# Attention and long convolution on one core: spacing row loads and instruction blocks in a planned order, with a landing wait on SyncE

## The chip, the core and the metric

The kernel runs on one core of a Trainium2 chip. Its engines work side by side, each through its own instructions in order: TensorE (PE; its weight loads are PEld in a profile), VectorE (DVE), ScalarE (ACT), GpSimd (POOL), and SyncE (SP), which here issues nearly all transfers. Semaphores tie them together. The metric is the device time of one execution in microseconds; lower is better.

## The reference

Two independent results are set side by side in one output of 2048 rows by 1024 columns.

```python
# left half: attention, 2048 positions, 32 heads of 16
qkv = x @ wqkv
p = softmax((q @ k.T) * 16 ** -0.5)          # per head
a = (p @ v) @ wo
# right half: gated long convolution, 512 channels
kv = shift(k, shift_k) * v                   # 4 taps per channel
y = irfft(rfft(pad(kv)) * rfft(pad(ssm_k)))[:2048]   # causal convolution over 2048 positions
b = q * (y + kv * ssm_D)
```

## The kernel before

**Attention.** Scores are made transposed, 128 keys by 512 queries at a time. Such a piece is a *block*; there are 2048 (4 query parts, 8 head groups, 16 key tiles, 4 heads at a time). The program walks through 695 *steps*. In each, TensorE makes the scores of two or three blocks (three in most, two in every other of the first 56 and in the last nine) into two alternating sets of three PSUM banks (`emit_qk`, the matmul at L762). ScalarE takes the exponential of all of them in one instruction (L769, 128x1536 for three blocks, 128x1024 for two). In 308 steps one block goes to VectorE and GpSimd instead, which build the exponential from integer arithmetic in *sets* of two or four blocks (L790 takes the block out of PSUM, L821 and L839 are GpSimd's pieces, L922 to L926 a polynomial, L889 or L894 the finish). TensorE then multiplies by the values (L971) into one of two banks.

**Convolution.** It is done by matmuls against shifted copies of the filter. The filter rows are laid out in a DRAM scratch, `kz_scratch`, and 256 KB of them serve one channel: that is one *row load*, `WR<-kz_scratch`. Four channels make a *quad*; 128 quads are worked off one after the other, each with four row loads into one of four buffers and 16 *lags* of four matmuls (`conv_lags`, L1157). Eight quads make a block of 32 channels, which TensorE then turns (L1178) and VectorE multiplies by q (L1188); after four of those a store goes out, and the next q columns are loaded (`QN`).

**The order.** Nothing is scheduled at run time. While the program is built, a planner in Python gives each engine a clock of its own, adds a duration for every instruction, and writes down each engine's list. Table constants at the top of the file steer it:

- `dve_choice` decides whether a step gives a block to VectorE: `LATE` and `OPEN_LATE` say how far VectorE may be behind, `OPEN_STEPS` how far apart sets are while all are pairs, `FIX_BEHIND` how far VectorE's clock may be past TensorE's, `LAST`, `PAIRS_AT_END` and `ROOM_END` rule the end.
- `V_DUE`, `X1_AT` and `X2_AT` set when the projections of values and queries are due.
- `run_conv` puts lags between score groups. The share that is due follows from what is left and from `CONV_END`. A piece is cut where `pe.stall` expects TensorE to run out of instructions: TensorE's list is taken to arrive in blocks of `FETCH` = 256, each `FETCH_US` after the last at the earliest.
- `load_wr` writes row loads into SyncE's list, one each `PACE` us of the plan's clock, or one each `PACE / 1.5` when more than six are waiting. A load carries a wait for the last TensorE instruction that had been planned then (`hold`), so that SyncE cannot issue it earlier, and for the quad that had used the buffer. The plan reckons when it lands from `START_US`, `SET_US` and `LAND_LATE`; `conv_ready` lets the lags of a quad into the plan only then.

SyncE's list is one queue: what stands behind a load that waits is issued after it.

Of the kernel before, what the change touches and what calls it, by code (L numbers as in the profile page):

```python
# [43 lines left out]
N_EARLY = 56  # L44
LAGS = 5
CONV_AT = 128
CONV_END = 640
TAIL = 18


# [12 lines left out]
TIME = 0.8  # L63
FULL = 4
APART = 2
OPEN_STEPS = 3
ROOM = {2: 4.0, 4: 8.0}
LATE = 9.0
CLOSE = 4.0
LAST = 6  # L70
ROOM_END = 1.5
PAIRS_AT_END = 20
PAIRS_AT = 4
OPEN_LATE = 4.5
DVE_OVER = 0.084
ACT_US = 0.425
ACT_OP = 0.066
DVE_SEEN = 0.12
FIX_BEHIND = 1.8
NEXT = -0.1  # L80
PV_HOLD = 3
LAG_US = 0.068
# [5 lines left out]
FILL_LATE = 0.5  # L88
HARD = 0.7
FETCH = 256  # L90
FETCH_AT = 192
FETCH_US = 4.0
EARLY = 6
ISSUE_US = 0.45
START_US = 2.0
# [4 lines left out]
SET_US = 0.72  # L100
# [3 lines left out]
KZ_AT = 11  # L104
KZ0_AT = 14
DG_AT = (1, 1, 7, 8)
V_DUE = -1
PACE = 0.95
FULL_PARTS = 6
KZ_LANDS = 24.2  # L110
KZ_OVER = 0.0
# [9 lines left out]
MUL_WAIT = 6  # L121
FINISH_RATE = 1.5
PASS_US = 3.0
X2_AT = 146
X1_AT = 166


class Count:
# [13 lines left out]
class Eng:  # L142
# [17 lines left out]
    def stall(self, n, us):  # L160
        (b, landed), late = self.fetch, 0.0
        while self.count + n > b:
            t = self.t + late + us * (b - self.count) / n
            late += max(0.0, landed - t)
            landed = max(landed, t) + FETCH_US
            b += FETCH
        return late, (b, landed)

    def op(self, fn, deps=(), inc=True, us=None, late=FILL_LATE, fill=False, counted=False):
        waits = []  # L170
        ready = max([0.0] + [self.at[(id(d[0]), d[1])] for d in deps if d])
        while self.fill and not fill and self.t + self.fill[0][0] <= ready + late:
            self.fill.pop(0)[1]()
        if inc and (self.sem, self.n) in deps:
            self.tied.add(self.n + 1)
        for d in deps:
            if d is None:
                continue
            sm, v = d
            self.t = max(self.t, self.at[(id(sm), v)])  # L180
            if self.seen.get(id(sm), 0) < v:
                self.seen[id(sm)] = v
                waits.append((sm, v))
        if counted:
            c = Count()
            fn(c)
            n = c.n + max(len(waits) - 1, 0)
            late, self.fetch = self.stall(n, us)
            self.t += late
            self.count += n  # L190
            self.counts = [x for x in self.counts if x[0] > self.t - RATE_US] + [(self.t, n)]
        self.t += (self.us if us is None else us) - (DVE_OVER if self.us == 0.69 else 0.0)
        self.last = [x for x in self.last if x[0] > self.t - SPAN] + [(self.t, self.us if us is None else us)]
        if inc:
            self.n += 1
            self.at[(id(self.sem), self.n)] = self.t + self.seen_after
        self.ops.append((waits, fn, self.sem if inc else None))
        return (self.sem, self.n)
# [21 lines left out]
def bass_concat_heads__mha_block__ssm_conv_h3__prompt_kernel(  # L220
# [21 lines left out]
    def sem(name):  # L242
        return enter(nc.semaphore(name))

    def sb(name, shape, dt=BF16):
# [36 lines left out]
    WR = [WRF[:, o:o + 4 * LROW].rearrange("p (c w) -> p c w", c=4)  # L282
          for o in (0, 4 * LROW + 64, 8 * LROW + 64, 12 * LROW + 96)]
# [15 lines left out]
    pe, act, dve, pool, sp = [Eng(sem(n), at, us, after) for n, us, after in (  # L299
        ("s_pe", 0.5, 0.11), ("s_act", 0.5, 0.16), ("s_dve", 0.69, DVE_SEEN), ("s_pool", 0.5, 0.1), ("s_sp", 0.05, 0.1))]  # L300

    queue = [0.0]

    def dma(eng, dsem, outp, inp, deps=(), transpose=False, us=4.0, takes=0.0):
        h = dsem.add()

        def fn(e):
            f = e.dma_start_transpose if transpose else e.dma_start
            f(outp, inp).then_inc(dsem.sem, 16)
        eng.op(fn, deps, inc=False, us=ISSUE_US if takes else 0.05)  # L310
        if takes:
            queue[0] = max(queue[0], eng.t + START_US) + takes
            us = queue[0] + 0.9 - eng.t
        at[(id(dsem.sem), dsem.n)] = eng.t + us
        return h
# [4 lines left out]
    def when_of(h):  # L320
        return at[(id(h[0]), h[1])] if h else 0.0
# [11 lines left out]
    d_wr = [DmaSem(sem(f"d_wr{i}")) for i in range(R_W)]  # L333
# [3 lines left out]
    wview = A_wqkv.rearrange("(c p) f -> p c f", p=128)  # L337
    h_x = {}
    h_x0 = dma(sp, d_x[0], KVE[:, 0:4, 0:C], x2[0:512, :].rearrange("(t p) d -> p t d", p=128))
    h_wq = [dma(act, d_w[0], WQ[:, :, 0:128], wview[:, :, 0:128])]  # L340
    h_wk = [dma(act, d_w[1], WK[:, :, 0:128], wview[:, :, D:D + 128])]

    def turn_in(dsem, dst, src, deps=(), us=4.0):
# [183 lines left out]
    h_kzt, h_kzs = [None], {}  # L527
# [56 lines left out]
    def k_part(r0, r1):  # L584
        def fn(e):
            ins = None
            for dc in range(4):
                ins = e.matmul(PS[:, 7, r0:r1], lhsT=WK[:, dc, 0:128], rhs=xT[:, dc, r0:r1], start=(dc == 0), stop=(dc == 3))
            return ins
        return pe.op(fn, h_x[0] + [h_wk[0], bank_free[7]], us=0.3 if r0 == 0 else 0.8)  # L590
    h = k_part(0, 128)
# [94 lines left out]
    def dve_choice(T):  # L686
# [3 lines left out]
        j = len(s.blks)  # L690
        if T + (s.k - j) * APART >= NT - LAST or not s.free() or dve.t > pe.t + FIX_BEHIND:
            return None
        behind = max(dve.t + sum(x[0] for x in dve_fill) + PASS_US * len(waiting) - pe.t, 0.0)
        if j == 0 and (behind > (LATE if h_kzall[0] else OPEN_LATE) or s.k == 2 and sets and T - sets[-1].at < OPEN_STEPS and T < FULL_AT) or j and T - s.at < APART * (s.k > 2):
            return None
        if len(rest_of[n]) / 3 < (ROOM[s.k] if T < NT - PAIRS_AT_END else ROOM_END) + APART * (s.k - 1 - j) + behind / 1.25:
            n = max(n + 1, 2)
# [411 lines left out]
    h_wr, h_qn, h_turn, h_yb = {}, {}, {}, {}  # L1109
# [6 lines left out]
    def load_wr(T):  # L1116
        while next_wr[0] < C // 4 and slots:
            qd = next_wr[0]
            next_wr[0] += 1
            r, h = slots.pop(0)  # L1120
            slot_of[qd] = r
            wr_parts.extend((qd, c, r, h) for c in range(4))
        while wr_parts:
            rate = max(RATE, sum(x[1] for x in pe.counts) / RATE_US)
            left = ((FETCH_AT - pe.count) % FETCH) / rate
            if pe.t < next_wr[1] or left < FETCH_NEAR and pe.t < next_wr[1] + 2 * FETCH_NEAR:
                return
            next_wr[1] = max(next_wr[1], pe.t - PACE) + (PACE if len(wr_parts) <= FULL_PARTS else PACE / 1.5)
            hold = [pe_last()] if next_wr[0] > 3 else []
            qd, c, r, h = wr_parts.pop(0)  # L1130
            src = bass.AP(tensor=kz_ap.tensor, offset=kz_ap[4 * qd + c, 0, 0].offset,
                          ap=[[NB * VG, 128 // VG], [LKZ, VG], [1, LROW]])
            h_wr[qd] = dma(sp, d_wr[r], WR[r][:, c, :], src, [h_kzs[i] for i in range(12, 16)] + [h] + hold, takes=SET_US)
            if c == 3:
                land[qd] = when_of(h_wr[qd]) + LAND_LATE

# [60 lines left out]
    def when(qb, g, kt, s=0):  # L1197
        return plan[blk_index[(qb, g, kt, s)]]
# [50 lines left out]
    def turn_job(b):  # L1249
        def job(T, bank):  # L1250
            def run():
# [11 lines left out]
    todo = [(when(0, 0, kt) + 1, x_at[kt // 4], n, unit_job("v", kt, 0, n)) for kt, n in [(0, 1), (1, 1)] + [(i, 2) for i in range(2, KT, 2)]]  # L1263
    todo += [(when(0, 4, kt) + V_DUE, when(0, 3, kt + 1, 3) + 4, 2, unit_job("v", kt, 1, 2)) for kt in range(0, KT, 2)]
    n_unit = 4 // UNIT
# [3 lines left out]
             for c in range(4) for j in range(4)]  # L1269
    todo += [(min(when(qb, 2 * o, 0) - 2 - EARLY, {1: X1_AT, 2: X2_AT}.get(qb, 999) + 8 * o), max(when(qb - 2, 2 * o + 1, 15, 3) + 6 if qb > 1 else 140 + 16 * (o // 2), 0),  # L1270
              n_unit, unit_job("q", qb, o)) for qb in range(1, NQB) for o in range(4)]
# [93 lines left out]
    def bg_step(T, lim):  # L1365
# [17 lines left out]
        if T >= N_EARLY:  # L1383
            st["lags"] = min(st["lags"] + rest / max(CONV_END - T, 1.0), 3.0 * LAGS)
        if run_jobs(T, lim):
# [58 lines left out]
    def pe_last():  # L1444
        return (pe.sem, pe.n)
# [186 lines left out]
```

## Time and profile before

| | us |
|---|---|
| runs | 809.6, 810.16, 813.01 |
| median | 810.16 |
| the profiled execution | 815.64 |
| its span, first to last instruction | 813.8 |
| ScalarE busy | 793.5 (98%) |
| VectorE busy | 771.1 (95%) |
| TensorE busy, matmuls | 704.0 (87%) |
| GpSimd busy | 369.6 (45%) |
| granted TensorE clock, mean | 0.993 |

The profile is one execution, taken apart by the hardware profiler. A group of instructions has its line in the program, its engine, what it writes and reads, how often it occurs, its busy time, and the idle time of the engine just before it with what ended that. L762 and so on are lines of the kernel before. The profiled execution has a time of its own, which is not that of the median run.

### The profile page before, as it was taken

Reading aid. Unit: us, or ns where it says so; the run is one execution under the profiler, and the core shown is the slowest. Engines: PE = TensorE matmul, PEld = TensorE weight load, DVE = VectorE, ACT = ScalarE, POOL = GpSimd, SP = SyncE. Lnnn points to the kernel's source line nnn. Section 1 sums busy time; section 2 is a strip of 40 time slices with the busy share of each in tenths; the row PEclk is TensorE's granted clock in tenths of the full one; section 3 lists DMA queues with packets and bytes.
Section 4 is the critical chain, followed back from the end, with each engine's and each line's share of the span. In section 5 each row is a group of like instructions: output and inputs, shape, how many; then the busy total and the mean of one; then the engine's idle time right before and its main releaser. Section 6 shows DMA issues by size and latency. Waiting matters only on the chain.

```text
span 813.8 us, 30354 instructions
## 1 busy us (share of the span) xinstructions
PE 704.0 (87%) x13322; PEld 317.5 (39%) x13356; DVE 771.1 (95%) x1160; ACT 793.5 (98%) x702; POOL 369.6 (45%) x453
## 2 busy tenths in 40 slices
PE   8988999888888888888888888888888879888887
PEld 3333334232344443434434444343444343344442
DVE  4999999999889999999999999999999989999997
ACT  6999999999999999999999999999999998999997
POOL 4322543465443354665364455455453444444440
PEclk9999999999999999999999999999999998999999
DMA  9976700214367876579878788688678788778851
GB/s 239 305 276 246 190 1 17 61 27 103 106 194 225 269 235 193 172 216 262 282 223 260 252 253 256 192 260 265 205 223 243 247 253 251 242 217 280 267 167 49
DMA packets 125012, 167.33 MB, mean 206 GB/s; under 512 B 50384, under 2 KB 57040, under 8 KB 124624
## 3 DMA queue, kind: packets, MB, share of 16 engines
q1 hardware_dynamic: 122480, 164.34, 66.3%
q8 instruction: 105, 1.72, 0.9%
q10 hardware_dynamic: 2400, 1.05, 0.6%
q14 instruction: 27, 0.22, 0.1%
HBM read 143.14 MB, written 16.52 MB: 196 GB/s over the span
## 4 chain that ended last, share of the span: by engine, by line
ACT 85%; PE 7%; DVE 6%; issue 1%; DMA 1%; DVEq 0%
ACT PT L769 85%; PE PS L762 2%; PE PS L971 1%; DVE EI L790 1%; DMA WR<-kz_scratch 1%; PE PS L1157 1%; PE PS L575 1%; DVE EA L926 1%; DVE EA L924 1%; PE PS L479 0%; PE PS L1082 0%; DVE WR L541 0%; DVE EI L889 0%; DVE KV L515 0%; DVE EA L925 0%
## 5 line engine op out<-in xcount | busy, mean ns | idle before, releaser
L769 ACT ACTIVATE PT<-PS 128x1024 bf16<-128x1024 f32 (+1 forms) x695 | 789.4, 1420 | 8.4 <-PE PS L762 7.9
L762 PE MATMUL PS<-QT,KTo 32*128 32x512 bf16 x2048 | 274.2, 387 | 92.1 <-ACT PT L769 62.3
L971 PE MATMUL PS<-PT,VAF 128*32 128x512 bf16 x1740 | 235.7, 391 | 0.2 <-DVE STG L1041 0.2
L1157 PE MATMUL PS<-WR,KV 128*6 128x64 bf16 (+15 forms) x8192 | 187.2, 213 | 5.6 <-issue 3.8
L1157 PEld LDWEIGHTS PS<-WR,KV 128*26 128x26 bf16 (+15 forms) x8192 | 150.2, 120 | 47.2 <-issue 25.6
L762 PEld LDWEIGHTS PS<-QT,KTo 32*128 32x128 bf16 x2048 | 70.5, 91 | 240.3 <-ACT PT L769 212.9
L790 DVE TENSOR_SCALAR EI<-PS 128x512 int32<-128x512 f32 x228 | 154.7, 681 | 7.0 <-PE PS L762 6.6
L821 POOL TENSOR_SCALAR xT<-EI 128x512 f16<-128x512 uint16 x84 | 78.0, 936 | 89.5 <-DVE xT L894 23.8
L839 POOL TENSOR_SCALAR EI<-EI 128x512 f16<-128x512 uint16 x100 | 76.6, 774 | 54.9 <-DVE EI L889 10.0
L821 POOL TENSOR_SCALAR STG<-EI 128x512 f16<-128x512 uint16 x74 | 64.4, 877 | 72.9 <-DVE EI L894 19.0
L971 PEld LDWEIGHTS PS<-PT,VAF 128*32 128x32 bf16 x1740 | 56.2, 93 | 83.7 <-issue 79.6
L790 DVE TENSOR_SCALAR xT<-PS 128x512 int32<-128x512 f32 x80 | 54.6, 682 | 3.1 <-PE PS L762 2.8
L971 PE MATMUL PS<-EI,VAF 128*32 128x512 bf16 x228 | 56.3, 389 | 0.2 <-DVE STG L1041 0.2
L821 POOL TENSOR_SCALAR STG<-xT 128x512 f16<-128x512 uint16 x34 | 31.5, 934 | 44.0 <-DVE EI L894 15.3
L1334 PE MATMUL PS<-ZR,IDN 128*128 128x512 bf16 (+3 forms) x192 | 51.0, 319 | 0.2 <-DVE EA L925 0.2
L821 POOL TENSOR_SCALAR xT<-xT 128x512 f16<-128x512 uint16 x37 | 31.7, 868 | 42.6 <-DVE EI L894 15.1
L894 DVE SCALAR_TENSOR_TENSOR EI<-EI,EA 128x1024 int16<-128x1024 uint16 (+1 forms) x46 | 46.5, 1022 | 0.3
L924 DVE TENSOR_TENSOR EA<-EA,xT 128x2048 f16<-128x2048 f16 x33 | 40.3, 1223 | 0.4
L926 DVE TENSOR_TENSOR EA<-EA,xT 128x2048 f16<-128x2048 f16 x33 | 40.4, 1223 | 0.2
L925 DVE TENSOR_SCALAR EA<-EA 128x2048 f16<-128x2048 f16 (+2 forms) x60 | 35.1, 586 | 0.8
L926 DVE TENSOR_TENSOR WKV<-WKV,STG 128x2048 f16<-128x2048 f16 x29 | 35.5, 1224 | 0.2
L924 DVE TENSOR_TENSOR WKV<-WKV,STG 128x2048 f16<-128x2048 f16 x29 | 35.3, 1218 | 0.3
(107 smaller groups left out, 700.6 us busy)
## 6 DMA issues: line engine op xcount, KB each, us to landing
WR<-kz_scratch SPq DMA_DIRECT2D x512, 256.0 KB, 3.8
kz_scratch<-WR SPq DMA_DIRECT2D x16, 752.0 KB, 4.5
QN<-in_B_q_dram SPq DMA_DIRECT2D x16, 128.0 KB, 3.5
out_dram<-KV SPq DMA_DIRECT2D x16, 128.0 KB, 4.1
out_dram<-OUTA SPq DMA_DIRECT2D x12, 128.0 KB, 2.7
QT<-in_B_ssm_k_dram SPq DMA_DIRECT2D x1, 1024.0 KB, 5.7
EI<-in_B_ssm_k_dram SPq DMA_DIRECT2D x1, 1024.0 KB, 7.7
STG<-in_B_v_dram SPq DMA_DIRECT2D x1, 1024.0 KB, 6.1
```

The costliest lines, as they stand in the source:

```text
L762: ins = e.matmul(PS[:, bank, :], lhsT=KTo[32 * s:32 * s + 32, g // 2, kt * 128:(kt + 1) * 128], rhs=QT[32 * s:32 * s + 32, qb % 2, g, :], ...
L769: h_exp[T] = act.op(lambda e: e.activation(PT[:, T % R_PT, 0:n * QB], PS[:, banks[0]:banks[0] + n, :].rearrange("p b f -> p (b f)"), ACT.E ...
L790: s.fix.append(dve.op(lambda e: e.tensor_scalar(ei_of(i)[:, 0, :], PS[:, bank, :], FIX_LO, FIX_ADD, ALU.max, ALU.add), [h] + old + [o.pv[i ...
L821: return e.tensor_scalar(out, src.bitcast(UINT16).rearrange("p i (f e) -> p i f e", e=2)[:, :, :, 0], FS / OCT, 0.0, ALU.mult, ALU.add)
L839: return e.tensor_scalar(out.bitcast(FP16)[:, :, 0:QB], src.bitcast(UINT16).rearrange("p i (f e) -> p i f e", e=2)[:, :, :, 1], FS, 0.0, A ...
L894: h = dve.op(lambda e: e.scalar_tensor_tensor(out, whole, FS, m, ALU.mult, ALU.add), [st[i] for i in range(k0, k1)], us=0.155 + 0.533 * (k ...
L924: step(2, lambda sl: lambda e: e.tensor_tensor(ea[:, sl], ea[:, sl], eb[:, sl], ALU.mult))
L925: step(4, lambda sl: lambda e: e.tensor_scalar(ea[:, sl], ea[:, sl], C1, 1.0, ALU.add, ALU.mult))
L926: step(2, lambda sl: lambda e: e.tensor_tensor(ea[:, sl], ea[:, sl], eb[:, sl], ALU.mult))
L971: ins = e.matmul(PS[32 * s:32 * s + 32, pvb(qb * NG + g), :], lhsT=VAF[:, kt, h * VW:h * VW + 32], rhs=rhs, start=(order[b] == 0), stop=(o ...
L1157: ins = e.matmul(PS[32 * c:32 * c + NW - 2 * n, BGB, col:col + 64], lhsT=KV[:, 2 * n:NW, 4 * qd + c], rhs=w, start=(n == 0), stop=(n == NB ...
L1334: return e.matmul(PS[:, bank, col:col + 128 * k], lhsT=IDN[:, :], rhs=ZR[:, :].rearrange("p (m d) -> p m d", m=1).broadcast_to([128, 4 * k ...
```

## The change

Two things change. Thirteen of the planner's constants get other values. The two in the change's name: `FETCH_US`, the least time between two blocks of TensorE's instructions, goes from 4.0 to 4.5, and `PACE`, between two row loads, from 0.95 to 1.1. The others concern the opening (`OPEN_STEPS`, `OPEN_LATE`, `V_DUE`, `X1_AT`, `X2_AT`), how far VectorE may lag (`LATE`, `FIX_BEHIND`), the end (`LAST`, `ROOM_END`, `PAIRS_AT_END`) and the convolution's end (`CONV_END`). And an engine's list can now hold a *soft* wait: it stands in the list and holds the engine on the chip, but the planner's clock does not know of it. `load_wr` uses it: a load of the first two channels of a quad waits until the quad two in front has landed, one of the last two until the quad one in front has.

```diff
-CONV_END = 640
+CONV_END = 647
-OPEN_STEPS = 3
+OPEN_STEPS = 4
-LATE = 9.0
+LATE = 10.0
-LAST = 6
-ROOM_END = 1.5
-PAIRS_AT_END = 20
+LAST = 5
+ROOM_END = 1.0
+PAIRS_AT_END = 18
-OPEN_LATE = 4.5
+OPEN_LATE = 5.0
-FIX_BEHIND = 1.8
+FIX_BEHIND = 1.6
-FETCH_US = 4.0
+FETCH_US = 4.5
-V_DUE = -1
-PACE = 0.95
+V_DUE = 1
+PACE = 1.1
-X2_AT = 146
-X1_AT = 166
+X2_AT = 144
+X1_AT = 162
...
     def op(..., soft=()):
...
+        for sm, v in soft:
+            if self.seen.get(id(sm), 0) < v:
+                self.seen[id(sm)] = v
+                waits.append((sm, v))
...
-            h_wr[qd] = dma(sp, d_wr[r], WR[r][:, c, :], src, [...] + [h] + hold, takes=SET_US)
+            h_wr[qd] = dma(sp, d_wr[r], WR[r][:, c, :], src, [...] + [h] + hold, takes=SET_US,
+                            soft=[h_wr[qd - 1 - (c < 2)]] if qd > 1 else [])
```

Lines are added by the change, so L762 is L766 in it, L1157 is L1162, L309 is L313. What it moves, at three places:

SyncE, the loads behind the fourth load of q columns (some 655 us in the profile before); `d_wr` is the landing of a row buffer. Before:

```order
L309 DMA WR<-kz_scratch 128x1x1024
L309 DMA QN<-in_B_q_dram 128x4x128 [waits s_dve]
L309 DMA QN<-in_B_q_dram 128x4x128 x3
L309 DMA out_dram<-KV 128x4x128
L309 DMA WR<-kz_scratch 128x1x1024 [waits s_pe] x4
L309 DMA out_dram<-KV 128x4x128
L309 DMA WR<-kz_scratch 128x1x1024 [waits s_pe] x5
L309 DMA out_dram<-KV 128x4x128
L309 DMA WR<-kz_scratch 128x1x1024 [waits s_pe] x4
L309 DMA WR<-kz_scratch 128x1x1024
```

Now:

```order
L313 DMA WR<-kz_scratch 128x1x1024 [waits d_wr2]
L313 DMA QN<-in_B_q_dram 128x4x128 [waits s_dve]
L313 DMA QN<-in_B_q_dram 128x4x128 x3
L313 DMA out_dram<-KV 128x4x128
L313 DMA WR<-kz_scratch 128x1x1024 [waits s_pe] x3
L313 DMA WR<-kz_scratch 128x1x1024 [waits d_wr3,s_pe]
L313 DMA out_dram<-KV 128x4x128
L313 DMA WR<-kz_scratch 128x1x1024 [waits s_pe] x2
L313 DMA WR<-kz_scratch 128x1x1024
L313 DMA WR<-kz_scratch 128x1x1024 [waits d_wr0,s_pe]
L313 DMA out_dram<-KV 128x4x128
L313 DMA WR<-kz_scratch 128x1x1024 [waits s_pe] x3
```

One load in four has got the landing wait, the third of its quad (the second pair's other load and the next quad's first two find that landing already waited for), and the stores of KV stand behind it; between two stores there are four row loads instead of four or five.

TensorE, where quad 117 begins (some 742 us before). Its lags fall from 32 columns to 2 within a quad. Before:

```order
L1157 MATMUL PS<-WR,KV 8x64 x4
L1157 MATMUL PS<-WR,KV 6x64 x4
L1157 MATMUL PS<-WR,KV 4x64 x4
L1157 MATMUL PS<-WR,KV 2x64 x4
L1157 MATMUL PS<-WR,KV 32x64 x4
L1157 MATMUL PS<-WR,KV 30x64 x4
L1157 MATMUL PS<-WR,KV 28x64 x4
L1157 MATMUL PS<-WR,KV 26x64 x4
L1157 MATMUL PS<-WR,KV 24x64 x4
L1157 MATMUL PS<-WR,KV 22x64 x4
L762 MATMUL PS<-QT,KTo 128x512 x3
L971 MATMUL PS<-PT,VAF 32x512 x2
```

Now:

```order
L1162 MATMUL PS<-WR,KV 8x64 x4
L1162 MATMUL PS<-WR,KV 6x64 x4
L1162 MATMUL PS<-WR,KV 4x64 x4
L1162 MATMUL PS<-WR,KV 2x64 x4
L1162 MATMUL PS<-WR,KV 32x64 x4
L1162 MATMUL PS<-WR,KV 30x64 x4
L1162 MATMUL PS<-WR,KV 28x64 x4
L1162 MATMUL PS<-WR,KV 26x64 x4
L1162 MATMUL PS<-WR,KV 24x64 x4
L1162 MATMUL PS<-WR,KV 22x64 x4
L766 MATMUL PS<-QT,KTo 128x512 x3
L975 MATMUL PS<-PT,VAF 32x512 x4
```

The last four lags of a quad and the first six of the next stand between two groups of scores in both; the row loads and the steps around them are spaced differently, the piece itself is not.

VectorE, the last sets before the closing transposes. Before:

```order
L925 TENSOR_SCALAR EA<-EA 128x2048
L926 TENSOR_TENSOR EA<-EA,xT 128x2048
L894 SCALAR_TENSOR_TENSOR EI<-EI,EA 128x2x512 x2
L821 TENSOR_SCALAR EA<-EI 128x512 x2
L922 TENSOR_SCALAR EA<-EA 128x512 x2
L924 TENSOR_TENSOR EA<-EA 128x512 x2
L925 TENSOR_SCALAR EA<-EA 128x512 x2
L926 TENSOR_TENSOR EA<-EA 128x512 x2
L894 SCALAR_TENSOR_TENSOR EI<-EI,EA 128x512 x2
L1061 STREAM_TRANSPOSE STG<-PS 128x256
```

Now:

```order
L929 TENSOR_SCALAR EA<-EA 128x512 x2
L930 TENSOR_TENSOR EA<-EA 128x512 x2
L898 SCALAR_TENSOR_TENSOR EI<-EI,EA 128x512 x2
L825 TENSOR_SCALAR xT<-EI 128x512
L926 TENSOR_SCALAR EA<-xT 128x2048
L928 TENSOR_TENSOR EA<-EA,xT 128x2048
L929 TENSOR_SCALAR EA<-EA 128x2048
L930 TENSOR_TENSOR EA<-EA,xT 128x2048
L898 SCALAR_TENSOR_TENSOR EI<-EI,EA 128x2x512 x2
L1065 STREAM_TRANSPOSE STG<-PS 128x256
```

Before, a set of four finished first and a pair came last; now the pair stands in front (out of sight here) and the set of four comes last.

Over the whole program ScalarE's list has 350 wide and 345 narrow exponentials in both, and VectorE's list 308 blocks in both.

More of the change, by code (lines that the diff above doesn't have):

```diff
@@ L167, in stall, with op @@
         return late, (b, landed)
-    def op(self, fn, deps=(), inc=True, us=None, late=FILL_LATE, fill=False, counted=False):
+    def op(self, fn, deps=(), inc=True, us=None, late=FILL_LATE, fill=False, counted=False, soft=()):
         waits = []
@@ L302, in bass_concat_heads__mha_block__ssm_conv_h3__prompt_kernel, with dma @@
     queue = [0.0]
-    def dma(eng, dsem, outp, inp, deps=(), transpose=False, us=4.0, takes=0.0):
+    def dma(eng, dsem, outp, inp, deps=(), transpose=False, us=4.0, takes=0.0, soft=()):
         h = dsem.add()
@@ L309, in fn @@
             f(outp, inp).then_inc(dsem.sem, 16)
-        eng.op(fn, deps, inc=False, us=ISSUE_US if takes else 0.05)
+        eng.op(fn, deps, inc=False, us=ISSUE_US if takes else 0.05, soft=soft)
         if takes:
@@ L1132, in load_wr @@
                           ap=[[NB * VG, 128 // VG], [LKZ, VG], [1, LROW]])
-            h_wr[qd] = dma(sp, d_wr[r], WR[r][:, c, :], src, [h_kzs[i] for i in range(12, 16)] + [h] + hold, takes=SET_US)
+            h_wr[qd] = dma(sp, d_wr[r], WR[r][:, c, :], src, [h_kzs[i] for i in range(12, 16)] + [h] + hold, takes=SET_US,
+                            soft=[h_wr[qd - 1 - (c < 2)]] if qd > 1 else [])
             if c == 3:
```

## The prediction

> **What bounds the kernel now.** I read the page first, for the engine that is never free.
>
> ```profile
> span 813.8 us, 30354 instructions
> ...
> PE 704.0 (87%) x13322; PEld 317.5 (39%) x13356; DVE 771.1 (95%) x1160; ACT 793.5 (98%) x702; POOL 369.6 (45%) x453
> ...
> L769 ACT ACTIVATE PT<-PS 128x1024 bf16<-128x1024 f32 (+1 forms) x695 | 789.4, 1420 | 8.4 <-PE PS L762 7.9
> ...
> q8 instruction: 105, 1.72, 0.9%
> ```
>
> ScalarE's exponentials fill 789.4 of 813.8 us, and of the 8.4 us they stand idle 7.9 go to waits for the score matmuls (L762). Nothing but those gaps, the opening and the end can become shorter unless ScalarE is given less work. The groups by shape say how much that is:
>
> ```profile
> L769 ACT ACTIVATE PT<-PS 128x1536 bf16<-128x1536 f32 x350 | 552.5, 1632 | 5.8 <-PE PS L762 5.5
> L769 ACT ACTIVATE PT<-PS 128x1024 bf16<-128x1024 f32 x345 | 400.2, 1204 | 2.6 <-PE PS L762 2.4
> ```
>
> Second, ScalarE's timeline, because it names every gap with its place:
>
> ```profile
> 9.63 11.62 ACT L769 ACTIVATE PT<-PS 128x1536 bf16<-128x1536 f32 x11 [0.75 <-PE PS L762]
> 21.54 2.86 ACT L769 ACTIVATE PT<-PS 128x1024 bf16<-128x1024 f32 x3 [0.28 <-PE PS L762]
> 24.56 7.37 ACT L769 ACTIVATE PT<-PS 128x1536 bf16<-128x1536 f32 x7 [0.16 <-PE PS L762]
> 32.23 9.14 ACT L769 ACTIVATE PT<-PS 128x1024 bf16<-128x1024 f32 x8 [0.29 <-PE PS L762]
> ...
> 57.53 4.25 ACT L769 ACTIVATE PT<-PS 128x1024 bf16<-128x1024 f32 x4 [0.31 <-PE PS L762]
> 62.02 1.02 ACT L769 ACTIVATE PT<-PS 128x1024 bf16<-128x1024 f32 x1 [0.24 <-PE PS L762]
> 63.21 5.13 ACT L769 ACTIVATE PT<-PS 128x1024 bf16<-128x1024 f32 x5 [0.16 <-PE PS L762]
> 69.05 92.21 ACT L769 ACTIVATE PT<-PS 128x1536 bf16<-128x1536 f32 x79 [0.71 <-PE PS L762]
> ...
> 669.98 2.48 ACT L769 ACTIVATE PT<-PS 128x1536 bf16<-128x1536 f32 x2 [1.66 <-PE PS L762]
> 672.90 2.37 ACT L769 ACTIVATE PT<-PS 128x1536 bf16<-128x1536 f32 x2 [0.44 <-PE PS L762]
> 676.26 2.53 ACT L769 ACTIVATE PT<-PS 128x1536 bf16<-128x1536 f32 x2 [0.99 <-PE PS L762]
> 679.61 66.53 ACT L769 ACTIVATE PT<-PS 128x1536 bf16<-128x1536 f32 x58 [0.82 <-PE PS L762]
> 746.36 4.65 ACT L769 ACTIVATE PT<-PS 128x1024 bf16<-128x1024 f32 x4 [0.22 <-PE PS L762]
> 751.85 54.85 ACT L769 ACTIVATE PT<-PS 128x1024 bf16<-128x1024 f32 x49 [0.85 <-PE PS L762]
> ```
>
> Four parts. The first exponential waits 0.75. The opening (21 to 69 us) loses 0.28 + 0.16 + 0.29 + 0.31 + 0.24 + 0.16 + 0.71 = 2.15. Then nothing for 600 us. Around 670 us 1.66 + 0.44 + 0.99 + 0.82 = 3.91 are lost, around 750 us 0.22 + 0.85 = 1.07. The last exponential ends at 751.85 + 54.85 = 806.70, and 7.1 us of closing work follow.
>
> Third, who made TensorE late at the two late places. The chain of waits and TensorE's timeline:
>
> ```profile
> 662.35 6.55 DMA WR<-kz_scratch
> ```
>
> ```profile
> 668.94 0.45 PE L1157 MATMUL PS<-WR,KV 128*32 128x64 bf16 x16 [1.68 <-DMA WR<-kz_scratch]
> 669.32 0.61 PE L762 MATMUL PS<-QT,KTo 32*128 32x512 bf16 x3
> ...
> 679.72 0.66 PE L1157 MATMUL PS<-WR,KV 128*32 128x64 bf16 x24
> 680.31 0.39 PE L762 MATMUL PS<-QT,KTo 32*128 32x512 bf16 x3
> ...
> 751.22 0.26 PE L1157 MATMUL PS<-WR,KV 128*4 128x64 bf16 x8 [1.52 <-issue]
> ```
>
> ```profile
> 670.00:680.00 10.00, 9.67 (x106) 2.77 (x106) 6.77 (x11) 7.68 (x7) 4.01 (x4) 0.53 0.90 265
> 740.00:745.00 5.00, 4.33 (x116) 2.07 (x114) 4.97 (x8) 5.00 (x6) 2.61 (x4) 1.00 1.00 316
> ```
>
> At 662.35 SyncE issued the last row load of a quad; it took 6.55 us and TensorE stood 1.68 us for it. Then the granted clock was 0.53 for ten microseconds (in these window rows the last three columns are granted clock, DMA share and GB/s), the score matmuls took 0.61 instead of 0.39, and that gave the 0.44, 0.99 and 0.82. At 751 TensorE waited 1.52 us for nothing that the profile shows ("issue"), just after a stretch in which the DMA engines were 100% busy. The page's instruction queue moved 1.72 MB in 105 pieces, 16 KB each, about one for every 254 of TensorE's matmuls and weight loads; I take the 1.52 for such a piece that came late.
>
> **The profiled run and the others.** It took 815.64, 1.8 around its span of 813.8. The timed runs are 809.6, 810.16 and 813.01, so the median is 5.5 lower. The two late places together are 3.91 + 1.07 = 4.98: without them the profiled run would be 810.7. Most runs evidently have little or none of either, and what the change can mend there is mostly not in the median. That is the main choice of this forecast: I start from 810.16, not from 815.64.
>
> **Part by part.** *Exponentials.* The changed order has the same 695 exponentials, 350 wide and 345 narrow, and 308 blocks on VectorE as before: 0. The floor follows: 813.8 less all 7.9 of waits is 805.9, with the 1.8 around it 807.7.
>
> *Late row loads and late instruction pieces (wider PACE and FETCH_US).* From nothing to the 0.56 between the median and the fastest run, since that is all of it that a median run can hold; I take −0.6, the whole, because both numbers move the plan away from the DMA's limit. Against it: at the quad near 750 us (quad 117) the new order puts as many lags (10) between two score groups as the old, so the wider spacing of the pieces thins nothing there. The Trainium skill (Runtime: NRT & Kernel Launch, Instruction fetch mechanics) says that a sequencer fetches its next 16 KiB block of 256 instructions while it runs the present one and that the crossing is mostly hidden. By that rule the wider spacing would be worth 0 and my sum 0.2 to 0.3 higher; the 1.52 us at 751 speaks against the rule wherever the DMA engines are full.
>
> *The new wait.* In the order it stands on the third load of each quad alone: the first two ask for a landing that the third load of the quad before has already waited for. So SyncE holds load three until the quad in front has landed whole. Its price comes from how long a load takes:
>
> ```profile
> WR<-kz_scratch SPq DMA_DIRECT2D x512, 256.0 KB, 3.8
> ...
> q1 hardware_dynamic: 4320, 4.70, 38.8%
> ...
> WR<-kz_scratch SPq DMA_DIRECT2D x16, 256.0 KB, 3.3
> ...
> WR<-kz_scratch SPq DMA_DIRECT2D x49, 256.0 KB, 4.1
> ...
> L309 SPq DMA_DIRECT2D WR<-kz_scratch x512: 512/602/2201, 85.9 to 781.1; - x171
> ```
>
> (All loads; the quiet stretch 187 to 230 us, where q1 holds 38.8% of the engines; the crowded 735 to 782; the issues' own time, median 602 ns.) The plan sets three loads after a quad's last one at 1.1 us each, 3.3 us, and a landing takes 3.3 to 4.1, so load three typically waits 0 to 0.8 us and load four follows 0.6 later, which eats most of that again. Behind it in SyncE's queue stand the next loads, the stores of KV and OUTA and, three times, the QN loads. The stores' readers are far off; the loads feed TensorE's lags. What covers a late load is the three quads in front of the one in use. TensorE has slack too:
>
> ```profile
> PE PS L762 <- ACT PT L769: 3.9, 13, 0.9
> ...
> 735.00:785.00 50.00, 19.63 (x873) 15.50 (x863) 1.00 0.87 275
> ```
>
> (Both from 735 to 785 us: waits of TensorE, and the lag matmuls alone.) A gain is possible as well: fewer loads in flight means each lands sooner, and the page's instruction pieces share the engines with fewer of them. I take +0.3, nearest to the cover; its ends are 0 and the +4.5 of the slow rival.
>
> *The opening* (V_DUE, OPEN_STEPS, OPEN_LATE). No operation is added; V units come two steps later, and one pair of blocks moves from step 52 to 54. The bounds are the 2.15 that are there: all gone, or as much again. I take −0.4, less than a fifth.
>
> *The end* (LAST, ROOM_END, PAIRS_AT_END). VectorE's last block moves one exponential earlier and a full set instead of a pair closes. VectorE stood idle there before its last transposes:
>
> ```profile
> 807.24 0.45 DVE L1061 STREAM_TRANSPOSE STG<-PS 128x256 f32<-128x256 f32 x1 [2.15 <-PE PS L971]
> ```
>
> Its 2.15 us cover the exchange; without that cover the closing would be longer by what VectorE is late, 0 to 1. I take 0.
>
> The sum: 810.16 − 0.6 + 0.3 − 0.4 = **809.5**.
>
> **Rivals.** *The gaps close (faster).* Opening and late places all go: fastest run 809.6 − 2.15 = 807.4. For it: planner numbers at both places were moved. Against: the first 48 steps give VectorE the same blocks as before.
>
> *The loads' rate becomes the bound (slower).* With the new wait a quad cannot be loaded faster than one landing plus one issue. At the end of the convolution the lags used 873 / 64 = 13.6 quads in 50 us, 3.67 us each. At 4.1 us a landing the wait allows one in 4.1 + 0.6 = 4.7, at 3.7 one in 4.3, at 3.3 one in 3.9. The middle costs 13.6 × 0.63 = 8.6 us, of which TensorE's 3.9 of slack hide their part: +4.7, time 814.2. It decides from a landing of 3.67 + 3.9 / 13.6 − 0.6 = 3.4 us on. For it: the median of all loads and that of the crowded stretch lie above that. Against: four loads at most stay in flight, and the buffers already full at the start of the stretch are not counted. A single repeat of the 670 us stall is the same mechanism at one place: 809.5 + 3.91 = 813.4. The Trainium skill (TensorE: Matmul & The Clock Gate, Part 1) has the clock fall after an idle window of about 3.4 us; here 1.68 us of waiting came before the 0.53. By the page such a stall would cost 1.66 and not 3.91; I keep the trace's sum.
>
> *It doesn't do what it says.* The wait never binds, because SyncE waits for TensorE anyway:
>
> ```profile
> SPq L309 <- PE PS L1157: 146.5, 142, 13.6
> SPq L309 <- PE PS L762: 108.8, 121, 5.7
> ```
>
> Then only the other numbers act, 810.2. The 3.8 us of the median landing against 3.3 speaks against it.
>
> **Chances.** Forecast 0.57 (its own range 808.3 to 811), gaps close 0.17, loads' rate 0.16, no effect 0.10. Half a percent, about what a measurement of this kernel can tell from no change, is 806.1 to 814.2. Below lies only a part of the second case, with the ScalarE floor at 807.7: 0.07. Above lies about half of the third and single stalls in the others: 0.13. The range reaches from the closed gaps to one stall, 807.4 to 813.4.
>
> **What would show it.** ScalarE's exponentials near 789 us in 695 pieces again; the third load of a quad in SyncE's queue waiting for a WR landing, some 0.5 us each; a median landing below 3.8; no 0.53 clock after the opening; the gaps of 21 to 69 us still about 2 us. I am wrong if L1157 waits for WR<-kz_scratch at several places, or if the closing exceeds 8 us because VectorE is late.

## The result, and the profile after

The changed kernel takes 841.0 us (median of six runs, 836.95 to 846.09), the kernel before 811.03 (six runs, 809.6 to 813.01): 3.7% slower, ratio 1.0367, 95% interval 1.0343 to 1.039. The forecast was 809.5. The profiled execution of the changed kernel took 841.46, with a span of 839.5 and a mean granted clock of 0.963. One run of the kernel before with the wait alone, of 851.54 us, was in a slower state and is left out of that kernel's numbers.

The page of the changed kernel: span, engines, the clock in 40 slices, the chain that ended last by engine, and three groups of instructions (busy time, mean ns of one, then idle time before them and what ended most of it).

```profile
span 839.5 us, 30462 instructions
...
PE 719.3 (86%) x13322; PEld 318.2 (38%) x13356; DVE 770.4 (92%) x1164; ACT 798.4 (95%) x702; POOL 364.8 (43%) x454
...
PEclk9999999999999999999799999999987968999989
...
ACT 69%; PE 12%; DMA 11%; DVE 7%; issue 1%; POOL 0%; DVEq 0%; SPq 0%; ACTq 0%
...
L773 ACT ACTIVATE PT<-PS 128x1536 bf16<-128x1536 f32 (+1 forms) x695 | 794.4, 1360 | 29.6 <-PE PS L766 28.5
...
L1162 PE MATMUL PS<-WR,KV 128*24 128x64 bf16 (+15 forms) x8192 | 193.3, 216 | 25.0 <-DMA WR<-kz_scratch 24.8
...
WR<-kz_scratch SPq DMA_DIRECT2D x512, 256.0 KB, 3.7
```

Two of these rows before the change, the clock and the chain:

```profile
PEclk9999999999999999999999999999999998999999
...
ACT 85%; PE 7%; DVE 6%; issue 1%; DMA 1%; DVEq 0%
```

The span grew by 839.5 − 813.8 = 25.7. ScalarE accounts for all of it: its 695 exponentials stand idle 29.6 us instead of 8.4, +21.2, and are busy 794.4 instead of 789.4, +5.0 with no instruction more; the first starts 0.5 earlier (9.15 against 9.63). Nearly all that idle time is ended by the score matmuls, as before, but the lag matmuls L1162 now stand 24.8 us for row loads, and DMA has 11% of the chain. The waits show the same from both sides, TensorE first (the kernel before in the first line) and then SyncE's queue (us in total, times, longest):

```profile
PE PS L1157 <- DMA WR<-kz_scratch: 1.7, 1, 1.7
...
PE PS L766 <- ACT PT L773: 51.2, 174, 0.9
PE PS L1162 <- DMA WR<-kz_scratch: 24.8, 22, 2.6
```

```profile
SPq L207 <- DMA WR<-kz_scratch: 144.6, 92, 3.1
SPq L313 <- DMA WR<-kz_scratch: 32.5, 19, 3.0
```

SyncE waited 111 times for a landing, 177.1 us in all, 1.6 us each; before there was no such wait. ScalarE's timeline says where it hurts (start, length, and in brackets the gap ahead):

```profile
9.15 11.62 ACT L773 ACTIVATE PT<-PS 128x1536 bf16<-128x1536 f32 x11 [0.75 <-PE PS L766]
...
140.11 269.32 ACT L773 ACTIVATE PT<-PS 128x1536 bf16<-128x1536 f32 x235 [0.19 <-PE PS L766]
410.25 1.02 ACT L773 ACTIVATE PT<-PS 128x1024 bf16<-128x1024 f32 x1 [0.82 <-PE PS L766]
...
674.75 1.02 ACT L773 ACTIVATE PT<-PS 128x1024 bf16<-128x1024 f32 x1 [1.88 <-PE PS L766]
...
697.28 2.92 ACT L773 ACTIVATE PT<-PS 128x1536 bf16<-128x1536 f32 x2 [2.22 <-PE PS L766]
...
814.64 17.76 ACT L773 ACTIVATE PT<-PS 128x1536 bf16<-128x1536 f32 x16 [0.68 <-PE PS L766]
```

The opening and the first 400 us are much as before. From 410 us on, where the kernel before ran clean until 670, there are gaps of up to 2.2 us; the row of the clock shows the worst of it in slices 30 to 34, some 610 to 715 us. The last exponential ends at 814.64 + 17.76 = 832.40, and 7.1 us of closing follow, as before.

What one such gap is made of, in the chain of waits of the changed kernel, then in TensorE's timeline, then in its windows (last three columns: granted clock, DMA share, GB/s):

```profile
669.76 3.75 DMA WR<-kz_scratch
673.55 0.61 PE PS L1162 x22
...
674.78 4.52 DMA WR<-kz_scratch
679.34 0.61 PE PS L1162 x27
```

```profile
673.55 0.61 PE L1162 MATMUL PS<-WR,KV 128*32 128x64 bf16 x28 [2.17 <-DMA WR<-kz_scratch]
674.10 0.61 PE L766 MATMUL PS<-QT,KTo 32*128 32x512 bf16 x3
...
679.34 0.61 PE L1162 MATMUL PS<-WR,KV 128*32 128x64 bf16 x28 [1.55 <-DMA WR<-kz_scratch]
```

```profile
670.00:680.00 10.00, 6.21 (x125) 2.74 (x122) 7.25 (x9) 6.26 (x6) 5.23 (x5) 0.65 0.82 227
680.00:690.00 10.00, 9.67 (x145) 3.09 (x143) 5.78 (x10) 8.52 (x7) 1.82 (x3) 0.66 0.70 174
```

A quad's fourth load goes out at 669.76 and lands 3.75 us later; TensorE has stood 2.17 us for it and starts that quad's lags 0.04 after the landing. The next quad goes the same way. No lead is left. The wait is not alone at the first of these quads: between its third load and its fourth stand four loads of q columns and a store, issued from 665.66 to 669.72. They stand there in the changed kernel without the wait too (the first experiment below), where this quad's fourth load went out 5.43 us ahead of its lags; here it is 3.79. Then the granted clock is 0.65 and 0.66 in the mean of the two stretches (1.00 from 665 to 670, 0.50 from 675 to 685), and a group of three score matmuls takes 0.61 instead of 0.39. The Trainium skill (TensorE: Matmul & The Clock Gate, Part 1) has the clock fall after an idle window of about 3.4 us; here the longest wait beside the fall is 2.17, so the trace does not agree with that figure.

### The profile page after: what moved, and what is told of

Read it like the earlier page. It is cut to its first block, busy times and chain, and to the rows that moved or that the text cites. A ratio compares the mean times of both kernels' runs of the same rounds, so it can differ in the third digit from the quotient of the medians.

```text
span 839.5 us, 30462 instructions
## 1 busy us (share of the span) xinstructions
PE 719.3 (86%) x13322; PEld 318.2 (38%) x13356; DVE 770.4 (92%) x1164; ACT 798.4 (95%) x702; POOL 364.8 (43%) x454
## 4 chain that ended last, share of the span: by engine, by line
ACT 69%; PE 12%; DMA 11%; DVE 7%; issue 1%; POOL 0%; DVEq 0%; SPq 0%; ACTq 0%
ACT PT L773 69%; DMA WR<-kz_scratch 10%; PE PS L766 4%; PE PS L975 3%; PE PS L1162 3%; DVE EI L794 1%; DMA kz_scratch<-WR 1%; PE PS L1339 1%; DVE EA L930 1%; DVE EA L928 1%; DMA KV<-in_A_x_dram 1%; DVE WR L545 0%; DVE xT L898 0%; DVE VAF L493 0%; PE PS L507 0%
## 5 line engine op out<-in xcount | busy, mean ns | idle before, releaser
L773 ACT ACTIVATE PT<-PS 128x1536 bf16<-128x1536 f32 (+1 forms) x695 | 794.4, 1360 | 29.6 <-PE PS L766 28.5
L766 PE MATMUL PS<-QT,KTo 32*128 32x512 bf16 x2048 | 280.3, 396 | 80.8 <-ACT PT L773 51.2
L975 PE MATMUL PS<-PT,VAF 128*32 128x512 bf16 x1740 | 240.0, 401 | 1.2 <-DVE STG L1045 0.9
L1162 PE MATMUL PS<-WR,KV 128*24 128x64 bf16 (+15 forms) x8192 | 193.3, 216 | 25.0 <-DMA WR<-kz_scratch 24.8
L1162 PEld LDWEIGHTS PS<-WR,KV 128*24 128x24 bf16 (+15 forms) x8192 | 150.4, 120 | 74.2 <-DMA WR<-kz_scratch 31.6
L766 PEld LDWEIGHTS PS<-QT,KTo 32*128 32x128 bf16 x2048 | 70.6, 91 | 225.5 <-ACT PT L773 184.8
L825 POOL TENSOR_SCALAR xT<-EI 128x512 f16<-128x512 uint16 x84 | 68.0, 817 | 109.4 <-DVE EI L898 31.5
L825 POOL TENSOR_SCALAR STG<-EI 128x512 f16<-128x512 uint16 x68 | 58.6, 870 | 96.8 <-DVE xT L898 32.5
L898 DVE SCALAR_TENSOR_TENSOR EI<-EI,EA 128x1024 int16<-128x1024 uint16 (+1 forms) x43 | 42.0, 983 | 0.2
L898 DVE SCALAR_TENSOR_TENSOR EI<-EI,WKV 128x1024 int16<-128x1024 uint16 (+1 forms) x36 | 37.9, 1059 | 0.1
L930 DVE TENSOR_TENSOR WKV<-WKV,STG 128x2048 f16<-128x2048 f16 x29 | 35.5, 1223 | 0.3
```

The lines of the kernel that those rows point to most:

```text
L766: ins = e.matmul(PS[:, bank, :], lhsT=KTo[32 * s:32 * s + 32, g // 2, kt * 128:(kt + 1) * 128], rhs=QT[32 * s:32 * s + 32, qb % 2, g, :], ...
L773: h_exp[T] = act.op(lambda e: e.activation(PT[:, T % R_PT, 0:n * QB], PS[:, banks[0]:banks[0] + n, :].rearrange("p b f -> p (b f)"), ACT.E ...
L825: return e.tensor_scalar(out, src.bitcast(UINT16).rearrange("p i (f e) -> p i f e", e=2)[:, :, :, 0], FS / OCT, 0.0, ALU.mult, ALU.add)
L898: h = dve.op(lambda e: e.scalar_tensor_tensor(out, whole, FS, m, ALU.mult, ALU.add), [st[i] for i in range(k0, k1)], us=0.155 + 0.533 * (k ...
L930: step(2, lambda sl: lambda e: e.tensor_tensor(ea[:, sl], ea[:, sl], eb[:, sl], ALU.mult))
L975: ins = e.matmul(PS[32 * s:32 * s + 32, pvb(qb * NG + g), :], lhsT=VAF[:, kt, h * VW:h * VW + 32], rhs=rhs, start=(order[b] == 0), stop=(o ...
```

## The experiments

All kernels compute the whole reference. Each differs from the changed kernel, or from the kernel before, only in what its diff shows. "Beside" is the median of the kernel before in the same comparison. Two theories stood at first: A, the new wait limits how fast the row loads come; B, the other spacing of the plan (the constants) does the harm.

**The constants alone.** The changed kernel without the wait.

```diff
-  soft=[h_wr[qd - 1 - (c < 2)]] if qd > 1 else [])
+  soft=[])
```

> The changed plan with all its new constants, but no load waits for a landing. Theory A (the wait caps the rate: a quad cannot be loaded faster than one landing, 3.7 us, plus one issue, 0.6, and the plan wants one every 4.5 us on average and every 3.7 in its dense stretches): without the wait TensorE waits under 3 us in all for WR<-kz_scratch instead of 24.8, and the time is 808 to 812, within 0.5% of before. Theory B (the new constants leave the loads too little lead, wait or no wait): over 825, with more than 10 us of waits of L1162 for WR<-kz_scratch.

Measured 809.79 (809.2 to 816.27), beside 812.47, ratio 0.9973 (0.9947 to 0.9998). Its group of exponentials and its waits of TensorE:

```profile
L773 ACT ACTIVATE PT<-PS 128x1536 bf16<-128x1536 f32 (+1 forms) x695 | 788.7, 1406 | 2.9 <-PE PS L766 2.4
```

```profile
PE PS L1162 <- DMA WR<-kz_scratch: 0.5, 1, 0.5
```

ScalarE's idle time goes from 29.6 to 2.9, its busy time from 794.4 to 788.7: 26.7 + 5.7 = 32.4 us, which covers the whole loss (the spans, 839.5 and 807.6, differ by 31.9). B falls: the constants do no harm, they gain a little. From here on the cost of a wait is the median less 809.8. The kernel before moved between 811.0 and 812.5 from one comparison to the next, so a cost of one or two microseconds can't be told from nothing.

**The wait alone.** The kernel before, its constants untouched, with the wait.

```diff
+  soft=[h_wr[qd - 1 - (c < 2)]] if qd > 1 else [])
```

> The plan of before with all its old constants, and the landing wait on the third load of each quad alone. Theory A: the plan of before wants its quads as densely (128 of them in about 510 steps), so the cap hits it too: 20 to 30 us of waits of the lags for WR<-kz_scratch and 825 to 845 us. Theory B: the wait alone does little, 810 to 814 us. A third way, that the two parts only hurt together, would lie between, 814 to 825.

Measured 844.58 (836.72 to 848.51), beside 812.47, ratio 1.0377 (1.03 to 1.0455); at the upper end of what theory A expected. The wait alone brings the loss, and the wider spacing does not soften it beyond the interval.

```profile
L1162 PE MATMUL PS<-WR,KV 128*20 128x64 bf16 (+15 forms) x8192 | 193.3, 216 | 31.6 <-DMA WR<-kz_scratch 28.3
```

**Where in the quad the wait stands.** Three versions of the changed kernel: the wait for the quad in front on the first load; on the fourth alone; and for the quad two in front, on the first.

```diff
+  soft=[h_wr[qd - 1]] if qd > 1 else [])                # first load
...
+  soft=[h_wr[qd - 1 - (c < 3)]] if qd > 1 else [])      # fourth load
...
+  soft=[h_wr[qd - 2]] if qd > 1 else [])                # two quads in front
```

> The changed plan, but the first load of each quad (so all four) waits until the quad in front has landed. Theory A gives a cycle of one landing plus three issues and gaps, 3.7 + 3 x 0.65 = 5.65 us a quad; some 124 quads from about 185 us on are then loaded by 185 + 124 x 5.65 = 886 us, and with 25 us from the last load to the end as now the time is 900 to 920 us. Theory B: the constants are what hurts, so 841 plus less than 20 us. If the loss came from stores and q loads held in SyncE's queue, it would grow with the added wait alone, to 845 to 860.

> The changed plan, but only the fourth load of each quad waits until the quad in front has landed; the third is free. Theory A: the cycle shrinks by one issue, to 3.7 + 0.05 = 3.75 us a quad, below the average of the plan and about at its dense stretches: most of the loss goes, 811 to 820 us. Theory B: nothing changes, 835 to 846 us.

> The changed plan, and every load waits for the landing of the quad two in front (which binds the first load of a quad alone). Theory A (cap by the wait): two quads per landing plus three issues, (4.2 + 1.95) / 2 = 3.1 us a quad, below the 3.7 of the dense stretches, so the wait costs nothing: 808 to 812, TensorE waits under 3 us for WR<-kz_scratch. A rival in which any landing wait in SyncE's list is what costs (SyncE wakes late, stores and q loads stand behind it): 815 to 830.

| wait binds on | median (range) | beside | ratio (95% interval) | cost against 809.8 |
|---|---|---|---|---|
| first load | 1049.6 (1046.79 to 1052.4) | 812.47 | 1.2916 (1.2839 to 1.2994) | 239.8 |
| third load (the change) | 841.0 | 811.03 | 1.0367 (1.0343 to 1.039) | 31.2 |
| fourth load | 815.53 (810.59 to 818.15) | 812.47 | 1.0037 (1.0011 to 1.0062) | 5.7 |
| two quads in front | 811.21 (808.78 to 813.45) | 811.79 | 0.9988 (0.9968 to 1.0008) | 1.4 |

The place in the quad decides between 5.7, 31 and 240 us; the second load was not tried. The fourth load and the two quads came out as expected, and with the latter the rival in which any landing wait in SyncE's list costs 5 us or more falls, as far as short waits go: SyncE waited 26 times there, 16.6 us in all. With the first load the direction was right, but 900 to 920 was expected. That kernel's page, SyncE's waits, and its chain:

```profile
L773 ACT ACTIVATE PT<-PS 128x1536 bf16<-128x1536 f32 (+1 forms) x695 | 811.6, 1279 | 223.7 <-PE PS L766 221.5
L1162 PE MATMUL PS<-WR,KV 128*10 128x64 bf16 (+15 forms) x8192 | 218.2, 227 | 178.0 <-DMA WR<-kz_scratch 177.7
```

```profile
SPq L207 <- DMA WR<-kz_scratch: 390.5, 108, 5.8
```

```profile
508.06 4.44 DMA WR<-kz_scratch
...
514.41 4.41 DMA WR<-kz_scratch
```

The landing that counts is that of the fourth load, which has three others just issued ahead of it: 4.4 us and not the 3.7 of the median load. From one such issue to the next pass 514.41 − 508.06 = 6.35 us, which is one landing and the three issues at 0.65 of the expectation, 4.4 + 1.95. From quad 8 on it is 6.57 in the mean, where 5.65 was expected: the landing was put too low.

**Which constants bring the small gain.** The kernel before with the two of the change's name; the changed kernel without the wait and without those two; the kernel before with the opening's three.

```diff
-FETCH_US = 4.0
-PACE = 0.95
+FETCH_US = 4.5
+PACE = 1.1
```

> The plan of before with two of the constants alone, FETCH_US 4.5 and PACE 1.1, and no landing wait. If the wider spacing is what made the plan without waits faster (809.8 against 812.5, ratio 0.997): 808 to 811, ratio 0.995 to 0.999, and fewer issue waits of the lags and fewer waits for WR<-kz_scratch than before. If the other constants made it: 811 to 814, ratio 0.999 to 1.003.

> The changed plan without the landing wait, with FETCH_US back at 4.0 and PACE at 0.95: the eleven other constants alone. If the wider spacing carries the gain: 811 to 814, with issue waits of some microseconds and a late load now and then as before. If the others carry it: 808 to 811.

```diff
-OPEN_STEPS = 3
-OPEN_LATE = 4.5
-V_DUE = -1
+OPEN_STEPS = 4
+OPEN_LATE = 5.0
+V_DUE = 1
```

> The plan of before with the three constants of the opening alone (OPEN_STEPS 4, OPEN_LATE 5.0, V_DUE 1), no wait. If they carry the gain of the other constants (ratio 0.9975): 808.5 to 811, ratio 0.996 to 0.999, the gap of 0.7 us at 69 us gone and nothing lost later. If the gain came from the convolution's and the end's constants: ratio 0.999 to 1.002.

`FETCH_US` and `PACE` alone: 811.83 (809.93 to 815.14), beside 811.79, ratio 0.9999 (0.9982 to 1.0017). The eleven others alone: 809.59 (808.16 to 811.4), beside 811.79, ratio 0.9975 (0.9959 to 0.9992). The opening's three alone: 813.74 (812.12 to 816.83), beside 811.95, ratio 1.0035 (1.0019 to 1.0051), with its gap of 0.70 still there at 66 us. So the wider spacing brings nothing that can be told, and the quarter of a percent comes from the eight constants that are left, or from these together with the opening's. Which of the eight stays open. In the kernel with the eleven, ScalarE's timeline has no gap from 139 us to the closing:

```profile
139.54 659.73 ACT L773 ACTIVATE PT<-PS 128x1536 bf16<-128x1536 f32 x579 [0.19 <-PE PS L766]
```

**The wait in one stretch only.** The changed kernel with the wait in the last 16 quads, the first 60, and those between.

```diff
+  soft=[h_wr[qd - 1 - (c < 2)]] if qd > 111 else [])
...
+  soft=[h_wr[qd - 1 - (c < 2)]] if 1 < qd < 60 else [])
...
+  soft=[h_wr[qd - 1 - (c < 2)]] if 59 < qd < 112 else [])
```

> The changed plan with the landing wait for the last 16 quads alone, the stretch on which the slow rival of the prediction rests. The prediction's own arithmetic gives +4.7: 814 to 815. The trace of the change has 5.5 us of load waits at these quads: 814 to 817. If a quad here is late only because the cap had already used up the lead further ahead: under 811.

> The changed plan with the landing wait for quads 2 to 59 alone. In the trace of the change the lags of these quads waited 2.5 us for loads. Theory A with local effect (each stretch pays for itself): 809.8 + 2.5 to 4 = 812 to 814. If the wait on the early quads uses up lead that the later ones need: over 820.

> The changed plan with the landing wait for quads 60 to 111 alone. In the trace of the change their lags waited 16.5 us for loads. If the stretches add up, this one and the first 60 make the rest of the loss: 841 - 809.8 - 5.3 = 26 together, so about 22 here: 829 to 835. If the loss needs all stretches together: under 822.

| wait in quads | median (range) | beside | ratio (95% interval) | cost against 809.8 |
|---|---|---|---|---|
| 112 to 127 | 815.07 (813.42 to 820.48) | 811.79 | 1.0044 (1.0024 to 1.0065) | 5.3 |
| 2 to 59 | 818.89 (817.8 to 819.66) | 811.95 | 1.009 (1.007 to 1.011) | 9.1 |
| 60 to 111 | 828.82 (827.8 to 832.11) | 811.95 | 1.022 (1.0198 to 1.0242) | 19.0 |

The sum is 33.4, the whole wait 31.2: what one stretch loses, no other wins back. The last 16 quads cost about what the prediction's slow rival had worked out for the end, 4.7, and those between about what was expected. The first 60 cost more than the local account expected and less than the other; the trace of that kernel shows it as waits of TensorE:

```profile
PE PS L1162 <- DMA WR<-kz_scratch: 9.5, 9, 2.3
```

**Every second quad.** By then A had become: the wait caps the rate at one landing and one issue a quad. The last run tells that apart from a price that each wait pays by itself (the two are called A and B in its expectation).

```diff
+  soft=[h_wr[qd - 1 - (c < 2)]] if qd > 1 and qd % 2 else [])
```

> The changed kernel with the landing wait in every second quad only (the odd ones); in the even quads no load waits for a landing. Two accounts of the 31.2 us that the wait costs over the whole program (841.0 against 809.8 without it) agree so far and part here. A, a cap on the rate: with the wait in every quad a quad takes at least one landing and one issue, some 4.3 us, against 4.5 that the plan wants on average, so what a pause loses is never made up. With the wait in every second quad, two quads take at least a landing and five issues, 3.7 + 5 x 0.6 = 6.7 us, 3.35 each, below even the 3.67 of the densest stretch: the leads come back behind each wait, and the cost all but goes, 810 to 815. B, a price per wait: each wait that binds delays its own quad's loads and that delay reaches TensorE by itself; half the waits cost half, 15.6 us, 822 to 829.

Measured 827.31 (824.61 to 830.95), beside 811.59, ratio 1.0181 (1.0142 to 1.022): 17.5 us, 56% of the whole. The cap as I had put it, with leads that come back as soon as the rate allows, is wrong; the wait in half the quads costs about half. (An odd quad has two waits here, since no even quad has waited for the landing two in front: its first load waits for that one, which by the run above costs next to nothing.) This kernel's waits in SyncE's queue, and the issues from 420 to 740 us (KB each, median us to landing):

```profile
SPq L207 <- DMA WR<-kz_scratch: 105.7, 68, 4.8
...
SPq L313 <- DMA WR<-kz_scratch: 11.0, 9, 3.5
```

```profile
WR<-kz_scratch SPq DMA_DIRECT2D x273, 256.0 KB, 4.0
```

77 waits of 1.5 us against 111 of 1.6. The row loads of this stretch number 264 with the wait in every quad, 273 here and 284 with none.

## Why the prediction was wrong, step by step

**The step that failed is the price of the new wait.** It was put at +0.3, on two sentences: load three "typically waits 0 to 0.8 us and load four follows 0.6 later, which eats most of that again", and "What covers a late load is the three quads in front of the one in use". The runs show +31.2 (841.0 against 809.8). The prediction's own sign of being wrong came with it: the lags (L1157, now L1162) wait for `WR<-kz_scratch` at several places, 22 times.

*The wait itself.* 1.6 us each, not 0 to 0.8. The 3.3 us between a quad's fourth load and the next third one was reckoned from `PACE`; in the trace of the kernel without the wait the median is 3.2, but a quarter of the loads come within 2.75. And the landing that counts is that of a fourth load, 4.2 in the median of the kernel before and 3.75 and 4.52 in the chain shown above, where 3.3 to 4.1 was taken.

*The cover.* This was, I take it, the larger mistake. A free buffer does not mean an early load: each load is held until TensorE reaches an instruction that the plan names (`hold`), and the plan sets it late. In the trace of the kernel without the wait I took, for quads 8 to 127, the time from the issue of the fourth load to the quad's first lag: median 7.7 us, a quarter below 6.0, a tenth below 5.3. A landing of about 4 leaves 1.3 to 3.7. A typical wait of 1.6 with single ones up to 3.1 takes that away in many quads. One quad in both traces, SyncE's and TensorE's timeline, first the kernel without the wait:

```profile
597.11 0.51 SPq L313 DMA_DIRECT2D WR<-kz_scratch  x1
...
602.57 0.33 PE L1162 MATMUL PS<-WR,KV 128*32 128x64 bf16 x12
```

then the changed kernel (the chain, and TensorE's timeline):

```profile
606.45 4.15 DMA WR<-kz_scratch
```

```profile
610.63 0.43 PE L1162 MATMUL PS<-WR,KV 128*32 128x64 bf16 x16 [0.76 <-DMA WR<-kz_scratch]
```

5.46 us from the last load to the lags without the wait, and 4.18 with it, which is the landing and nothing more. And because the later loads are held to TensorE's instructions, they slide with TensorE: the lead does not come back. That would be why the stretches add up; no run takes `hold` out, so this step is argued and not shown. With buffers four quads deep the changed plan had a cover of one to four microseconds. The trace of before, where I could have read it, has leads of 9.7 in the median, a quarter below 7.7 and a tenth below 6.0, which less 4.2 for a fourth load's landing is a cover of 2 to 5.5. The lead does not set the price by itself: the kernel before had more of it, and the wait alone still cost it 32 us. With the wait its median lead falls from 9.7 to 6.9, that of the changed plan from 7.7 to 6.0; waits in quad after quad use up a longer lead as well.

*A reckoning of it.* I took the issue times and first lags of the kernel without the wait, let a load land 3.7 us after its issue but no sooner than 0.95 after the one before it, put in the wait, and slid everything later by what TensorE was late. That gives 29.8 us for the third load, 241 for the first, 0 for two quads in front, 6.9, 7.2 and 14.4 for the three stretches (measured 31.2, 239.8, 1.4, 5.3, 9.1 and 19.0). The two numbers were chosen afterwards, and at 3.3 and 0.87 the third load would cost 1.8: the price is that steep in the landing time. It gives only 5.9 for every second quad and nothing for the fourth load, where 17.5 and 5.7 were measured, so it supports the account and does not prove it. With 4.0, the median landing in the row of every second quad above, it would give 13.8 there. From the issue times of the kernel before it gives 25.5 for the third load, where the wait alone measured 32. In the kernel with every second wait single waits grow to 4.8 us, where the changed kernel had at most 3.1; whether that makes up the missing 12 us stays open.

**The slow rival** ("The loads' rate becomes the bound", chance 0.16) had the right place, the wait in SyncE's queue, and sign. It was applied to the last 13.6 quads alone, for +4.7, and there the run gave +5.3. It took for granted that elsewhere the plan is slower than the cap. That fails, as the issues of the kernel before from 420 to 740 us show:

```profile
WR<-kz_scratch SPq DMA_DIRECT2D x281, 256.0 KB, 3.9
```

4 × 320 / 281 = 4.56 us a quad, hardly more than the cap of 4.3 at a landing of 3.7. But a cap alone is not the mechanism either: every second quad would then be free.

**"Fewer loads in flight means each lands sooner"** was the gain set against it. The median landing of all loads went from 3.8 to 3.7 us, and with the first load waiting it is 3.5. For the load that counts, the fourth, it fell from 4.2 to 3.7. So the gain is there, but half a microsecond does not pay for waits of 1.6.

**The clock.** The prediction had counted on no fall after the opening. The clock's own record in the trace of the changed kernel has seven stretches at 0.50 from 410 us to the closing, of 3.4 to 13.7 us and 61 us in all; the kernel before has one until its closing, of 10.2 us, and the changed kernel without the wait none. They begin during or shortly after stands of 0.76 to 2.63 us for a row load, but not every stand brings one: after that of 1.55 us which ends at 656.92 the clock stays at 1.00 until 670. How much of the 32.4 us at ScalarE is the stands themselves and how much the slower matmuls behind them, no run separates; TensorE's waits for loads come to 24.8.

**What held.** The 695 exponentials, the opening's gaps, the closing of 7.1 us, and that the wait binds on the third load. Without the wait the sum was 809.2 and the run gave 809.79, but that is luck and not the reason given: the −0.6 was for wider `PACE` and `FETCH_US`, which measure 0.9999 (0.9982 to 1.0017), and the −0.4 for the opening, which alone measures 1.0035. The other constants, put at nothing, carry it.

**A version ahead of both** is the changed kernel without the wait: 0.9973 (0.9947 to 0.9998) with all constants, 0.9975 (0.9959 to 0.9992) with the eleven.

## What to carry to other kernels

Before a wait is added to an issuing queue, read from the trace how long before its use each transfer is issued, and compare that lead, less the landing, with the wait; the number of buffers does not tell it when the issue itself is held to the progress of the engine that uses the data. A wait for a transfer two groups in front cost nothing here, for the one just in front 6, 31 or 240 us by its place in the group. And where issues are held to their consumer, do not count on delays being won back: here the costs of the three stretches added up to the whole (33.4 against 31.2), so count the wait in every group, not in the busiest stretch alone. The Trainium skill (DMA: Bandwidth & Descriptors, Rules for kernel authors) says to issue a DMA early and wait on its semaphore late; the change issues later because it waits earlier, and its 31.2 us agree with the rule.

## What the runs showed of the hardware

A landing wait turns spaced loads into bursts, and in these traces a load lands later the further back it stands in its burst. The median of all 256 KB loads hardly moves: 3.8 us in the kernel before, 3.7 with the third load waiting and 3.5 with the first. Taken by place from quad 8 on (at least 60 landings of each on record), the load that waited lands soonest: with the first load waiting the four take 3.1, 3.3, 3.9 and 4.2 us. With the third waiting, it takes 3.3, the fourth 3.7, and the next quad's first and second, right behind them, 3.8 and 4.1; in the kernel before the four of a quad take 3.7, 3.7, 3.8 and 4.2. The DMA engines are not full meanwhile: with the first load waiting their share from 400 to 900 us is 0.56 (the last but one number):

```profile
400.00:900.00 500.00, 364.47 (x6895) 150.45 (x6892) 331.60 (x455) 347.76 (x294) 160.80 (x182) 0.73 0.56 168
```

The same 695 exponentials are busy 788.7 us with gaps of 2.9 us in all between them and 794.4 with gaps of 29.6; with gaps of 223.7 it is 811.6. Consecutive ones overlap in these records (695 of 1406 ns make 977 us), and each gap takes one overlap away (the mean falls from 1406 to 1360 and 1279 ns); that this is the cause is read from the numbers and was not tried.
